# RWKV attention with a mixture of experts: five units' x on ScalarE and GpSimd, and eight half splits of w1 moved later

## The chip, the cores and the metric

The kernel runs on one core of one Trainium2 chip. The metric is the device time of one execution in microseconds (us); the time of a kernel is the median of several runs.

## The reference

First a linear recurrence per head (4 batches, 8 heads, 768 steps, head size 48), then a top-1 mixture of 8 experts on its output (3072 tokens of 384 columns, hidden size 1024):

```
y[t]  = r[t] . (state + (u*k[t]) outer v[t]);   state = w[t]*state + k[t] outer v[t]
x     = y as (tokens, 384)
e     = argmax(x @ w_gate + modality_bias[modality_id]);   g = its softmax value
out   = g * (relu(x @ w1[e]) @ w2[e])
```

## The kernel before

**The recurrence.** The 3072 tokens are 24 units of 128 tokens (6 per batch). `att_iter(i)` (L281) is one turn of a software pipeline over i = -2 to 23, called at L831: it prepares unit i+2 (two scans on VectorE at L289 and L292; two products on GpSimd, K at L240 and G at L300; r copied into PSUM by ScalarE at L234 and multiplied on VectorE at L237), does the scores and the state of unit i+1 (TensorE transposes K at L314, ScalarE copies the result to KT at L316, TensorE forms the scores pS at L338, VectorE masks them into A at L340, TensorE computes G's row sums at L271 into the tile pT, ScalarE rescales the state at L246 and L249), and forms y of unit i in the PSUM tile pY (L365, L377, L380). With i it also turns the finished y of unit i-1 into x (`x_rows`, L403), and transposes x of unit i-2 for the gate's logits (`x_cols`, L427 and ScalarE's copy xT at L428; `logits`, L433).

Each engine runs its own instructions strictly in the order in which the program issues them, so a wait of one holds up everything behind it on that engine. Order is set by hand; there is no planner.

**x_rows** adds two terms: y in PSUM and dV in SBUF (GpSimd's product of L296). It has two forms. By default VectorE adds them in one instruction (L417). With `by_two`, which only iterations 2 and 3 use before the change, ScalarE copies y to SBUF (L414) and GpSimd adds dV in place (L415), since the addition reads SBUF alone.

**The splits.** Each expert matrix is used as a sum of two reduced-precision parts: `wh` is the rounded copy (ScalarE), `wl` the rest (raw minus wh, on GpSimd or VectorE). For the first block of tokens, whose expert e0 is known early, w1 is loaded in 8 pieces (L843) into `raw[0]` and split in 16 halves by `w_split_half(n)` (L225): half n belongs to piece n // 2, and is one ScalarE cast of 128x192 (L228) and one GpSimd subtraction (L229). Before the change two halves are done in each of the iterations 7 to 10 (pieces 0 to 3), four in iteration 22 and the last four after iteration 23.

**The experts.** Tokens are scattered to rows sorted by expert (L632) and worked on in blocks of up to 512 (`seq`, L891; the loop at L892). For a block q and each of the 8 pieces f, `blk_up` (L696) runs nine 512-column matmuls (L702) on piece f of wh[0] and wl[0] into one of two PSUM tiles, pS0 and pS1, in turns (q = 0), then a relu on ScalarE (L711) and the rest on VectorE (L713); the tile is free for piece f+2 when both have read it. `blk_down` (L717) follows. Between the pieces, `w_split` (L220) splits the matrices to come: a cast of two pieces on ScalarE (L222) and a subtraction on VectorE or GpSimd (L223).

**The load of the second block.** `blk_raw(1, 0)` (L863) loads the second block's w1 into `raw[0]` in two halves (pieces 0 to 3, pieces 4 to 7), issued by SyncE. It reads the expert's number and a flag from a table (L643, L644), which VectorE finishes with L572; the loads carry that flag as a condition and move nothing if the expert is that of the block before, but are issued, and are waited for, all the same. Whatever reads a part of `raw[0]` after them in the program waits for the load of that half.

```
        if i == NU - 1:
            for n in done:
                w_split_half(n)
...
    blk_raw(1, 0)
...
        for f in range(FC):
            s = 2 * FC * q + f
            blk_up(q, f)
            if q == 0 and f % 2 == 0:
                w_split(1, f // 2)
            if q != 1 and f % 2 and nxt < HO:
                w_split(0, f // 2)
```

Of the kernel before, what the change touches and what calls it, by code (L numbers as in the profile page):

```python
# [20 lines left out]
NU = B * NCH  # L21
# [37 lines left out]
def kernel(ctx: ExitStack, tc: tile.TileContext, rkw, vt, wf, cst, mid, wg, bias, w1, w2, out):  # L59
# [165 lines left out]
    def w_split_half(n):  # L225
        f, c = n // 2, n % 2 * (DM // 2)
        part = lambda t: t[:, f, c:c + DM // 2]
        nc.scalar.copy(out=part(wh[0]), in_=part(raw[0]))  # L228
        nc.gpsimd.tensor_tensor(out=part(wl[0]), in0=part(raw[0]), in1=part(wh[0]).bitcast(F32), op=ALU.subtract)  # L229
# [46 lines left out]
    hooks = []  # L276
    done = iter(range(2 * FC))

    SPLITS = {**{i: 2 for i in range(7, 11)}, NU - 2: 4}

    def att_iter(i):  # L281
        a, m, z = i + 2, i + 1, i
# [15 lines left out]
        if ok(a):  # L298
            mk_k(a, k)
            nc.gpsimd.tensor_tensor(out=wt(a, "G", [P, 512]), in0=r, in1=k, op=ALU.mult)  # L300
        for _ in range(SPLITS.get(i, 0)):
            w_split_half(next(done))
        if ok(z - 1):
            x_rows(z - 1, i in (2, 3))
        last = first(m + 1)
        if ok(m):
            K, R, v = T["K", m], T["R", m], T["v", m]
# [95 lines left out]
    def x_rows(n, by_two=False):  # L403
        c, j = part(n)
        if j == 0:

            T["xp", c] = (rt if c else xa).tile([P, NJS[c], 400], F32, tag="xp", name=f"xp{c}", bufs=1)
        if n == 0:
            T["R"] = pt("x", "pR")

            nc.tensor.matmul(out=T["R"][:, 511:512], lhsT=wm[:, 0:P], rhs=wm[:, 0:1], start=True, stop=True, skip_group_check=True)
        x, dV = T["xp", c][:, j, 0:DM], T["dV", n].rearrange("p a b -> p (a b)")
        if by_two:
            nc.scalar.copy(out=x, in_=T["py", n][:, 0:DM])  # L414
            nc.gpsimd.tensor_tensor(out=x, in0=x, in1=dV, op=ALU.add)  # L415
        else:
            nc.vector.tensor_tensor(out=x, in0=T["py", n][:, 0:DM], in1=dV, op=ALU.add)  # L417

    def part(n):
        c = n >= CUT[1]  # L420
        return int(c), n - CUT[c]
# [274 lines left out]
    def blk_up(q, f):  # L696
        xh, xo = (t[:, :, 0:width(q)] for t in X["x", q][0:2])
        pp = pt(f"u{q}_{f}", UPB[(q * FC + f) % 3] if isinstance(q, int) and q else f"pS{f % 2}", (P, BT))[:, 0:width(q)]
        n = 0
        for c in range(KC):  # L700
            for wsrc, xsrc in ((wh, xh), (wh, xo), (wl, xh)):
                nc.tensor.matmul(out=pp, lhsT=wsrc[0][:, f, c * P:(c + 1) * P], rhs=xsrc[:, c], start=(n == 0), stop=(n == 3 * KC - 1))  # L702
                n += 1
        w = width(q)
        h2 = bp["h"].tile([P, 2 * BT], F32R, tag="h2", name=f"h{q}_{f}", bufs=FC)
        hh, hl = h2[:, 0:w], h2[:, BT:BT + w]
        cuts = ((0, w, BT),)
        if w % P:
            wf = w - w % P
            cuts = ((wf, w, w), (0, wf, BT))  # L710
        nc.scalar.activation(out=hh, in_=pp, func=AF.Relu)  # L711
        for c0, c1, o in cuts:
            nc.vector.scalar_tensor_tensor(out=h2[:, o:o + c1 - c0], in0=pp[:, c0:c1], scalar=0.0, in1=hh[:, c0:c1].bitcast(F32), op0=ALU.max, op1=ALU.subtract)  # L713
        X["h", q, f] = (hh, hl)
        X["hx", q, f] = h2
# [103 lines left out]
    for i in range(-2, NU):  # L819
        if 2 <= i < 7:  # L820
            hooks.append((setup_a, setup_b, setup_c, setup_d, setup_e)[i - 2])
        if i == CUT[1] + 1:
            ra, tb = route_a(0), table(0)
            hooks.extend([lambda: list(ra), lambda: hook_b(0)])
        if i == CUT[1] + 2:
            route_x(0)
        if i >= NU - 2:
            hooks.append(lambda n=1 + 2 * (i == NU - 1): [next(tb, None) for _ in range(n)])
        if i == NU - 1:
            prep.close()  # L830
        att_iter(i)  # L831
        if i == NU - 1:
            for n in done:
                w_split_half(n)
        if i != -1 and ok(i + 3):
            loadv(max(i + 3, 2))
        if ok(i + 6):
            load(i + 6, ((1024, 1541),))
        if i == 4:
            e0 = nc.sync.value_load(e0i[0:1, 0:1], min_val=0, max_val=E - 1)  # L840
        for n in range(2 * FC):
            if i == (n + 4 if n < FC // 2 else NU - 10 + n if n < FC else NU - 6 + (n - FC) // 2):
                w_raw(e0, n // FC, n % FC, parts=FC)  # L843
        if ok(i + 6):
            load(i + 6, ((0, 1024),))
        if i == -1:
            clear((ersb, 0.0), (onesb, 1.0), (one8, 1.0), (mfx, 0.0), (rbx, 0.0))
        if i == 0:
            clear((zt, 0.0), (zt[:, DM:DM + 1], 1.0), (zt[:, DM + 1:DM + 2].bitcast(I32), PAD_ID), (glo, W_LO), (ghi, -W_HI))
            setup_0()  # L850
        if i == 0:
            early()
        if i == 4:
            r0 = nc.sync.value_load(e0r[0:1, 0:1], min_val=0, max_val=(E - 1) * RS)
        if 8 <= i < 8 + JT:
            rows_apart("xz", nc.sync.dma_start(out=xs[ds(r0 + (i - 8) * P, P), :], in_=zt))

        drain(1)
        if i == NU - 3:
            assert not pend  # L860
            blk_load(0)
# [30 lines left out]
    for n, q in enumerate(seq):  # L892
        nxt, nxt2 = (seq[n + d] if n + d < len(seq) else None for d in (1, 2))
        if q >= HO:
            for k in range(2):
                half_up(q, k)
                if n == NQ and k == 0:
                    blk_out(NQ - 1, (JT - 1,))
            if nxt is not None:
                half_t(nxt)  # L900
            half_down(q)
            if nxt is not None:
                blk_out(q, (0,))
            continue

        load = blk_load if nxt < HO else half_load
        if q > 1:
            load(nxt)
        for f in range(FC):
            s = 2 * FC * q + f  # L910
            blk_up(q, f)
            if s == 2:
                logits(NU - 1)
            if q == 0 and f % 2 == 0:
# [3 lines that stand above are left out]
            if s == 4:  # L918
                list(route_a(1))
            if s == 5:  # L920
                route_x(1)
            if s == 6:
                hook_b(1)
            if q == 1 or s == FC - 1:
                drain(1, lambda h: nc.gpsimd.tensor_copy(out=pj, in_=h), X["h", q, f][0])
            if q == 1 and f > 3:
                if f > 4:
                    nc.gpsimd.tensor_copy(out=pj, in_=X["h", q, f][0][0:1, 0:1].bitcast(F32))
                late.pop(0)()
            if q == 1 and f < 2:  # L930
                blk_raw(nxt, f)
            if q == 1 and f == 5:
                assert not pend
                load(nxt)
            tend(s)
        if n == len(seq) - 2:
            bad, end, endh, rest = (nc.values_load(flg[0:1, i:i + 1], min_val=lo, max_val=hi)
                                    for i, lo, hi in ((0, 0, P), (1, NQ, HO), (2, HO + NH, NTAB), (3, 0, P + 1 + NTAB)))
        if q == 0:
            blk_raw(1, 1)  # L940
        if q >= NA and nxt2 is not None:
            blk_raw(nxt2, 0)
        for f in range(FC):
            s = 2 * FC * q + FC + f
            blk_down(q, f)
            if f == 0:
                (blk_t if nxt < HO else half_t)(nxt)
            if q == 1 and f % 2 == 0:
                w_split(0, f // 2)
            if f % 2:  # L950
                w_split(1, f // 2, eng=nc.vector if q in (0, NQ - 1) else None)
            if q == 2 and f in (3, 5):
                next(tab1)
            if q == 0:
                drain(1, lambda h: nc.gpsimd.memset(h, 0.0), X["h", q, f][0])
                if f == 1:
                    tab1 = table(1)
                if f in (1, 4, 6):
                    next(tab1)
                if f == 1:  # L960
                    pad_rows()
            tend(s)
        if q == 1:
            blk_raw(nxt2, 0)
        if q >= 1 and nxt2 is not None:
            blk_raw(nxt2, 1)
        blk_out(q, range(width(q) // P), late=late if q == 0 else None)
        if q == NQ - 1:
            blk_sum(q)
# [190 lines left out]
```

## Time and profile before

| what | value |
|---|---|
| median of 3 runs | 338.92 us (338.17 to 339.05) |
| the profiled execution: its own time | 338.15 us |
| its span in the trace | 336.40 us |
| TensorE (PE) busy | 323.6 us |
| VectorE (DVE) busy | 215.9 us |
| ScalarE (ACT) busy | 204.3 us |
| GpSimd (POOL) busy | 190.7 us |
| recurrence / experts, by the first matmul of line 702 | 0 to 124.1 us / 124.1 us to the end |

The busy times are averages over two stages with different limits: in the recurrence four engines work side by side, in the experts TensorE has nearly all the work. In the rows below, a line of a timeline gives the start in us, the length of one instruction or of several merged ones (x2 and so on), the engine, the line of the program, the operation, and in brackets how long the engine had been idle and what released it.

### The profile page before, as it was taken

Reading aid. Unit: us, or ns where it says so; the run is one execution under the profiler, and the core shown is the slowest. Engines: PE = TensorE matmul, PEld = TensorE weight load, DVE = VectorE, ACT = ScalarE, POOL = GpSimd, SP = SyncE. Lnnn points to the kernel's source line nnn. Section 1 sums busy time; section 2 is a strip of 40 time slices with the busy share of each in tenths; the row PEclk is TensorE's granted clock in tenths of the full one; section 3 lists DMA queues with packets and bytes.
Section 4 is the critical chain, followed back from the end, with each engine's and each line's share of the span. In section 5 each row is a group of like instructions: output and inputs, shape, how many; then the busy total and the mean of one; then the engine's idle time right before and its main releaser. Section 6 shows DMA issues by size and latency. Waiting matters only on the chain. (4 is left out here: it accounts for less than half of the span.)

```text
span 336.4 us, 10136 instructions
## 1 busy us (share of the span) xinstructions
PE 323.6 (96%) x3943; PEld 293.6 (87%) x3943; DVE 215.9 (64%) x381; ACT 204.3 (61%) x462; POOL 190.7 (57%) x221
## 2 busy tenths in 40 slices
PE   7999999999999999999999999999999999999993
PEld 3788989988899897899889988997899889999993
DVE  6999999999999655795333965933560464054230
ACT  3997799787498845542521867638745855642150
POOL 7989889689999925676461680255024703450041
PEclk9999999999999999999999999999999999999998
DMA  7998898877998432425346037026544773260010
GB/s 252 410 362 247 268 305 261 276 249 224 302 312 247 154 92 96 94 95 214 142 146 184 0 82 250 0 72 169 183 166 164 205 239 96 94 211 5 0 74 31
DMA packets 35586, 58.66 MB, mean 174 GB/s; under 512 B 17297, under 2 KB 22089, under 8 KB 35528
## 3 DMA queue, kind: packets, MB, share of 16 engines
q1 hardware_dynamic: 32424, 48.45, 45.8%
q0 software_dynamic: 3104, 9.47, 7.5%
q8 instruction: 33, 0.54, 0.7%
q14 instruction: 25, 0.20, 0.2%
HBM read 57.86 MB, written 12.67 MB: 210 GB/s over the span
## 5 line engine op out<-in xcount | busy, mean ns | idle before, releaser
L223 POOL TENSOR_TENSOR wl<-raw,wh 128x768 fp32r<-128x768 f32 x20 | 38.9, 1951 | 74.8 <-ACT wh L222 74.7
L222 ACT CAST wh<-raw 128x768 fp32r<-128x768 f32 x48 | 39.3, 832 | 38.9 <-PE pU_d L724 23.0
L713 DVE SCALAR_TENSOR_TENSOR h<-pS_u,h 128x512 fp32r<-128x512 f32 (+2 forms) x39 | 23.1, 608 | 39.3 <-ACT h L711 39.0
L744 POOL DMA_INDIRECT out<-ot,xg x24 | 24.3, 1011 | 30.7 <-ACT ot L753 25.2
L702 PE MATMUL pS_u<-xh,wh 128*128 128x512 f32 (+1 forms) x102 | 39.8, 390 | 0.8 <-DVE h L713 0.8
L223 DVE TENSOR_TENSOR wl<-raw,wh 128x768 fp32r<-128x768 f32 x28 | 31.0, 1113 | 14.6 <-ACT wh L222 14.3
L702 PE MATMUL pS_u<-xo,wh 128*128 128x512 f32 (+1 forms) x102 | 39.2, 384 | 0.0
L702 PE MATMUL pS_u<-xh,wl 128*128 128x512 f32 (+1 forms) x102 | 39.2, 384 | 0.0
L711 ACT ACTIVATE h<-pS_u 128x512 fp32r<-128x512 f32 (+1 forms) x34 | 19.7, 586 | 27.7 <-PE pS_u L702 25.6
L724 PE MATMUL pX_d<-wh,h 128*128 128x384 f32 x96 | 32.3, 337 | 0.0
L724 PE MATMUL pY_d<-wh,h 128*128 128x384 f32 x96 | 32.2, 335 | 0.0
L724 PE MATMUL pK_d<-wh,h 128*128 128x384 f32 x96 | 32.1, 334 | 0.0
L240 POOL TENSOR_TENSOR K<-in,B 128x512 f32<-128x512 f32 x24 | 28.5, 1186 | 6.1 <-PE pK L314 2.3
L632 POOL DMA_INDIRECT xs<-xp,posT x24 | 26.1, 1089 | 9.5 <-issue 7.1
L300 POOL TENSOR_TENSOR G<-in 128x512 f32<-128x512 f32 x24 | 30.6, 1276 | 0.0
L289 DVE TENSOR_TENSOR_SCAN B<-in,pX_d 128x516 f32<-128x516 f32 x24 | 29.3, 1219 | 1.7 <-DMA in<-rkw 1.7
L292 DVE TENSOR_TENSOR_SCAN E<-in,pX_d 128x516 f32<-128x516 f32 x24 | 29.5, 1229 | 0.8
L724 PE MATMUL pU_d<-wh,h 128*128 128x384 f32 x80 | 26.7, 334 | 0.0
L713 DVE SCALAR_TENSOR_TENSOR h<-pT_u,h 128x512 fp32r<-128x512 f32 (+2 forms) x17 | 9.5, 576 | 24.2 <-ACT h L711 24.2
L380 PE MATMUL pY<-v,A 128*64 128x48 f32 x368 | 25.1, 222 | 0.0
L246 ACT ACTIVATE pU_st<-pU_st,B 128x48 f32<-128x48 f32 x80 | 22.0, 275 | 2.8 <-PE pU_st L352 0.4
L380 PEld LDWEIGHTS pY<-v,A 128*64 128x64 f32 x368 | 23.7, 138 | 0.0
(237 smaller groups left out, 861.6 us busy)
## 6 DMA issues: line engine op xcount, KB each, us to landing
raw<-w SPq DMA_DIRECT2D x24, 768.0 KB
in<-rkw SPq DMA_DIRECT2D x23, 512.0 KB
v<-vt SPq DMA_DIRECT2D x24, 288.0 KB
in<-rkw SPq DMA_DIRECT2D x23, 258.5 KB
wg<-wf SPq DMA_DIRECT2D x8, 576.0 KB
xl<-xs SPq DMA_DIRECT2D x20, 192.0 KB
raw<-w SPq DMA_DIRECT2D x16, 192.0 KB
xs<-zt SPq DMA_DIRECT2D x12, 193.0 KB
```

Of the source, the lines that this page charges most:

```text
L222: nc.scalar.copy(out=wh[k][:, sl], in_=raw[k][:, sl])
L223: (eng or (nc.vector, nc.gpsimd)[k]).tensor_tensor(out=wl[k][:, sl], in0=raw[k][:, sl], in1=wh[k][:, sl].bitcast(F32), op=ALU.subtract)
L240: nc.gpsimd.tensor_tensor(out=wt(a, "K", [P, 4, P]), in0=quarters(k), in1=quarters(T["B", a][:, 1:517])[:, :, 1:129], op=ALU.mult)
L289: nc.vector.tensor_tensor_scan(out=Bt[:, 516:0:-1], data0=w[:, 516:0:-1], data1=d1[:, 516:0:-1], initial=0.0, op0=ALU.mult, op1=ALU.max)
L292: nc.vector.tensor_tensor_scan(out=Et, data0=w[:, 0:516], data1=d1[:, 1:2].to_broadcast([P, 516]), initial=1.0, op0=ALU.mult, op1=ALU.max)
L300: nc.gpsimd.tensor_tensor(out=wt(a, "G", [P, 512]), in0=r, in1=k, op=ALU.mult)
L380: nc.tensor.matmul(out=yh[64:P, g, sw, hh], lhsT=A[:, hh, g, 1 + sw], rhs=vs[:, g, hh] if sw else v[:, h * D:(h + 1) * D], start=new and n ...
L632: rows_apart("xs", nc.gpsimd.indirect_dma_start(out=xs[:, :], out_offset=bass.IndirectOffsetOnAxis(ap=posT[:, n:n + 1], axis=0), in_=T["xp ...
L702: nc.tensor.matmul(out=pp, lhsT=wsrc[0][:, f, c * P:(c + 1) * P], rhs=xsrc[:, c], start=(n == 0), stop=(n == 3 * KC - 1))
L713: nc.vector.scalar_tensor_tensor(out=h2[:, o:o + c1 - c0], in0=pp[:, c0:c1], scalar=0.0, in1=hh[:, c0:c1].bitcast(F32), op0=ALU.max, op1=A ...
L724: nc.tensor.matmul(out=X["y", q][j], lhsT=hsrc[:, j * P:(j + 1) * P], rhs=wsrc[1][:, f], start=(f == 0 and n == 0), stop=(last and n == 2))
L744: ins = nc.gpsimd.indirect_dma_start(out=out[:, :], out_offset=bass.IndirectOffsetOnAxis(ap=xg[0:n, j, 1:2].bitcast(I32), axis=0), in_=ot[ ...
```

## The change

Iterations 7 to 11 (which form x of units 6 to 10) use the two-instruction form of `x_rows`. The eight half splits of iterations 7 to 10 go away there. Iteration 22 and the end of the recurrence keep four each, but these are now halves 0 to 7 (pieces 0 to 3); halves 8 to 15 (pieces 4 to 7) are done four behind `blk_up(0, 0)` and four behind `blk_up(0, 1)`. The load of L863 now stands ahead of these eight in the program.

```
-    SPLITS = {**{i: 2 for i in range(7, 11)}, NU - 2: 4}
+    SPLITS = {NU - 2: 4}
+    BY_TWO = (2, 3, 7, 8, 9, 10, 11)
...
         if ok(z - 1):
-            x_rows(z - 1, i in (2, 3))
+            x_rows(z - 1, i in BY_TWO)
...
         if i == NU - 1:
-            for n in done:
-                w_split_half(n)
+            for _ in range(4):
+                w_split_half(next(done))
...
             blk_up(q, f)
+            if s < 2:
+                for _ in range(4):
+                    w_split_half(next(done))
             if s == 2:
                 logits(NU - 1)
```

## Rows read from the trace of the kernel before

**Rows 1.** The page's part 1: busy us (share of the span) xinstructions.

```profile
PE 323.6 (96%) x3943; PEld 293.6 (87%) x3943; DVE 215.9 (64%) x381; ACT 204.3 (61%) x462; POOL 190.7 (57%) x221
```

**Rows 2.** Timeline of VectorE, iterations 7 and 8.

```profile
42.65 1.22 DVE L289 TENSOR_TENSOR_SCAN B<-in,pX_d 128x516 f32<-128x516 f32 x1
...
47.17 1.22 DVE L289 TENSOR_TENSOR_SCAN B<-in,pX_d 128x516 f32<-128x516 f32 x1
...
49.79 0.53 DVE L417 TENSOR_TENSOR xp<-pY,dV 128x384 f32<-128x384 f32 x1
```

**Rows 3.** Timeline of TensorE: iterations 7, 10, 13, 21 and 22.

```profile
43.39 0.66 PE L314 MATMUL pK<-cs,K 128*128 128x128 f32 x4
...
45.35 0.63 PE L271 MATMUL pT<-cs,G 128*64 128x2 f32 x16
...
57.91 0.55 PE L427 MATMUL pT<-cs,xp 128*128 128x128 f32 x3
...
74.93 0.88 PE L365 MATMUL pY<-SPb,R 128*64 128x96 f32 x16 [0.28 <-DVE xp L417]
...
109.75 0.66 PE L314 MATMUL pK<-cs,K 128*128 128x128 f32 x4
...
114.46 0.55 PE L427 MATMUL pT<-cs,xp 128*128 128x128 f32 x3
```

**Rows 4.** Timeline of ScalarE, iterations 7 and 8.

```profile
43.60 0.60 ACT L228 CAST wh<-raw 128x192 fp32r<-128x192 f32 x2
...
44.72 0.48 ACT L428 COPY xT<-pT 128x384 f32<-128x384 f32 x1
...
48.43 0.60 ACT L228 CAST wh<-raw 128x192 fp32r<-128x192 f32 x2
```

**Rows 5.** Timelines of ScalarE and GpSimd, iteration 2, which has the two-instruction form.

```profile
20.42 0.48 ACT L414 COPY xp<-pY 128x384 f32<-128x384 f32 x1
...
23.44 1.01 POOL L415 TENSOR_TENSOR xp<-xp,dV 128x384 f32<-128x384 f32 x1
```

**Rows 6.** Timeline of GpSimd, iteration 7: the two subtractions of its splits.

```profile
46.38 1.15 POOL L229 TENSOR_TENSOR wl<-raw,wh 128x192 fp32r<-128x192 f32 x2
```

**Rows 7.** Timeline of ScalarE: iteration 22, then the first pieces of the experts.

```profile
114.64 1.11 ACT L228 CAST wh<-raw 128x192 fp32r<-128x192 f32 x4
...
126.50 0.60 ACT L711 ACTIVATE h<-pS_u 128x512 fp32r<-128x512 f32 x1 [0.95 <-POOL wl L229]
127.00 0.83 ACT L222 CAST wh<-raw 128x768 fp32r<-128x768 f32 x1
128.49 0.60 ACT L711 ACTIVATE h<-pS_u 128x512 fp32r<-128x512 f32 x1 [0.67 <-PE pS_u L702]
129.52 0.83 ACT L222 CAST wh<-raw 128x768 fp32r<-128x768 f32 x1 [0.43 <-DMA raw<-w]
```

**Rows 8.** Waits of SyncE's queue: us in total, times, longest.

```profile
SPq L643 <- DVE fA L572: 10.6, 1, 10.6
```

**Rows 9.** Timeline of SyncE's queue: the two halves of the load of L863.

```profile
129.43 0.09 SPq L217 DMA_DIRECT2D raw<-w  x1
...
129.96 0.08 SPq L217 DMA_DIRECT2D raw<-w  x1
```

**Rows 10.** Timeline of VectorE, pieces 1 and on of the first block.

```profile
129.12 0.69 DVE L713 SCALAR_TENSOR_TENSOR h<-pS_u,h 128x512 fp32r<-128x512 f32 x1 [0.50 <-ACT h L711]
130.39 0.96 DVE L223 TENSOR_TENSOR wl<-raw,wh 128x768 fp32r<-128x768 f32 x1 [0.58 <-ACT wh L222]
```

**Rows 11.** Timeline of TensorE: the first matmuls of pieces 3 and 4.

```profile
131.39 0.50 PE L702 MATMUL pS_u<-xh,wh 128*128 128x512 f32 x1
...
133.57 0.39 PE L702 MATMUL pS_u<-xh,wh 128*128 128x512 f32 x1
```

**Rows 12.** Timelines of VectorE and GpSimd, splitting at the same time, later in the experts.

```profile
188.55 2.01 DVE L223 TENSOR_TENSOR wl<-raw,wh 128x768 fp32r<-128x768 f32 x1 [0.51 <-ACT wh L222]
...
187.86 1.88 POOL L223 TENSOR_TENSOR wl<-raw,wh 128x768 fp32r<-128x768 f32 x1 [9.63 <-ACT wh L222]
```

## The prediction

> **What bounds the kernel now.** I read the page's busy times first: TensorE is busy for 96% of the span [rows 1]. That alone doesn't say that it is the limit in the recurrence, where matmuls are small and VectorE is full too. So I went to the timelines of the single engines, over the iterations that the change touches, and then over the first microseconds of the experts.
>
> VectorE takes 47.17 - 42.65 = 4.52 us for an iteration, without a gap, and 0.53 us of it is the addition that the change takes away [rows 2]. Read alone, that says that VectorE is the limit and that each iteration of the five would give back 0.53 us. But TensorE is slower still: between 43.39 and 57.91 it does iterations 7, 8 and 9, so 14.52 / 3 = 4.84 us each, where an iteration that nothing disturbs (21) takes 114.46 - 109.75 = 4.71 us [rows 3]. VectorE can be slower or faster than that for an iteration; over a batch it keeps up because TensorE has less to do at a batch's first and last unit.
>
> Why 4.84 and not 4.71 is in ScalarE's timeline: with its two casts of the splits it needs 48.43 - 43.60 = 4.83 us per iteration, back to back [rows 4]. Its copy xT ends at 44.72 + 0.48 = 45.20, and TensorE's next group, L271 into the same PSUM tile, starts at 45.35, right behind it [rows 3, 4]. So in iterations 7 to 9 ScalarE, by way of xT, holds TensorE up by about 0.13 us each. In the experts TensorE is the limit: what holds it up there reaches the end, since it has next to no idle time left there that could take a delay up.
>
> **The change part by part.**
>
> *The x of iterations 7 to 11.* VectorE loses five additions, 5 x 0.53 = 2.65 us [rows 2]. ScalarE loses two casts of 0.60 us together [rows 4] and gains a copy of 0.48 us [rows 5]: 4.83 - 0.60 + 0.48 = 4.71 us, which is just TensorE's own pace. In iteration 11, where there were no casts, the copy is new, but iteration 10 closes a batch, so ScalarE has neither KT nor a state to rescale in it and is ahead. GpSimd gains an addition of 1.01 us [rows 5] and loses two subtractions of 1.15 us [rows 6], so nothing. pY is read earlier than now (the copy stands early in ScalarE's order, VectorE's addition behind both scans), so the write of the next pY waits no longer than before; nothing speaks for a loss here.
>
> What TensorE gets out of it: 14.52 - 3 x 4.71 = 0.39 us from iterations 7 to 9. VectorE, which then runs ahead as far as the scores let it, arrives earlier at iteration 13, where TensorE waited 0.28 us for the addition of L417 [rows 3]; that wait goes too. Sum: **0.7 us gained**. Bounds: 0, if the copy makes ScalarE as late as the casts did; 2.65, if VectorE were the limit after all. I take 0.7, since TensorE's 4.71 us is a measured floor of a full iteration. What is late next is TensorE itself.
>
> *The splits that stay at the end of the recurrence.* Four in iteration 22 and four behind iteration 23, as before, only of other pieces, which were loaded long ago: no change.
>
> *The splits that move behind blk_up(0, 0) and blk_up(0, 1).* Their own work is small: four casts take 1.11 us [rows 7], and TensorE needs some 2 us for a piece. The cost is a wait. In the program the load of the second block's w1 now stands ahead of them, and pieces 4 to 7 are its second half. SyncE reads the table for that load only when VectorE has finished it [rows 8], so the two halves are issued at 129.43 and 129.96 and done at about 130.04 [rows 9]. That even a load that moves nothing is waited for is seen before the change: the cast of pieces 0 and 1 starts at 129.52, right when the first half is done, after a wait of 0.43 us put down to that DMA [rows 7]. Now four casts of pieces 4 and 5 wait for the second half from 127.00 on, and behind them, on the same engine, the relu of piece 1.
>
> Step by step, in the old trace's time (records of ScalarE follow each other some 0.1 us before the end of the one in front: relu 126.50 with 0.60, next 127.00 [rows 7]):
> 1. The four casts start at 130.04 and end at 131.15; the cast for w2 (0.83) ends at 131.98; the relu of piece 1 starts at about 131.9, where it started at 128.49 [rows 7].
> 2. VectorE's part of piece 1 starts 129.12 - 128.49 = 0.63 us behind its relu and takes 0.69 [rows 7, 10]: it ends at 133.22. Only then is pS1 free for piece 3, which TensorE began at 131.39 [rows 11]: **a stall of 1.8 us**.
> 3. Piece 3 takes 133.57 - 131.39 = 2.18 us from such a start [rows 11], until 135.40. Meanwhile ScalarE goes from the relu (next start 132.4) through four casts (133.5) and the cast of pieces 0 and 1 for the next block (134.33). VectorE does the subtraction of that one, 0.96 [rows 10], until 135.3, and then its part of piece 2, 0.69, until 136.0. TensorE's piece 4 needs pS0: it begins at 136.0 and not at 135.40, **0.6 us more**. Against 133.57 that is 2.43 us late, and with a second restart (a first matmul takes 0.50 behind a gap, 0.39 without one [rows 11]) 2.5 us.
> 4. Piece 5 needs the relu of piece 3, which ScalarE can do once TensorE is through with it, at about 135.5: with 0.63 and 0.69 behind it, 136.9, before piece 4 ends at about 138.1. From here on nothing is late. The second four casts, at 132.4, have their load long done, and piece 6 comes two pieces behind piece 4, after 140.
>
> GpSimd has eight subtractions more here, of 1.15 / 2 = 0.58 us each [rows 6], and VectorE's subtraction of step 3 falls among them. Later in the trace, where both engines split at once, VectorE's instruction takes 2.01 us where it takes 0.96 us alone [rows 10, 12]: it ends 0.8 us behind GpSimd's, which began first and ended at 189.74. So step 3 can grow by what is left of one subtraction of GpSimd, 0 to 0.58; I take the middle, **0.3**. The Trainium skill, page "SBUF — State Buffer", section "Who interferes with whom", states it as a rule: a VectorE instruction with two SBUF inputs and a GpSimd instruction that reads SBUF shut each other out, and the one that came second waits for the whole of the first. These rows agree; with it the sum is 2.1, without it 1.8.
>
> **Sum:** 1.8 + 0.6 + 0.1 + 0.3 - 0.7 = **2.1 us slower**. Against the profiled execution's own time that is 338.15 + 2.1 = 340.25. That execution lies 0.77 us under the median of the runs shown, so I put it on the median: 338.92 + 2.1 = **341.0**. A measurement of this kernel can tell about 0.3%, 1.0 us, from no change.
>
> **The rivals.**
>
> *The splits don't wait* (not slower). If the casts of pieces 4 and 5 could go at 127.00, they and the cast for w2 would end at 128.9, the relu of piece 1 would be 0.4 us later than 128.49, VectorE's part would end at 130.2 and piece 3 would begin at 131.39 as now. Then only the gain is left: 338.92 - 0.7 = 338.2, no change. It decides from the point where the load is done before 127.7. For it: the two issues are only 0.08 and 0.09 us long [rows 9]. Against: the wait of 0.43 us [rows 7], and the flag that comes from VectorE's last table instruction. Chance 0.12.
>
> *VectorE is the limit of the recurrence*, and all of 2.65 us comes back, at the same stall of 2.8: 338.92 + 0.15 = 339.1, no change. For it: VectorE has no gap in 4.52 us. Against: 4.71 us of TensorE. If in part, between 339.1 and 341.0. Chance 0.09 for what ends below 1.0 us.
>
> *Both at once*: 338.92 - 2.65 = 336.3, faster. Chance 0.04.
>
> *The copy is no cheaper than the casts*: gain 0 and 2.8 of stall, 341.7; this is still my case, and its upper end with 0.3 more for the shut-out is 342.0.
>
> **How the numbers follow.** My case has 0.75, with a range of its own from the first stall alone less the gain, 338.92 + 1.8 - 0.7 = 340.0, to 342.0. For 8 in 10 the range goes down past the second rival's 339.1 toward the first, and takes 0.4 more above for the spread of the runs shown: 338.6 to 342.4. Slower 0.75, same 0.19 (first rival 0.12, second rival's part 0.07), faster 0.06 (the third, and 0.02 of the others' spread).
>
> **What would show it.** Right: in the changed kernel TensorE's iterations 7 to 9 take 4.71 us; the first cast of L228 in the experts follows the second load's issue, with the DMA as what released it; TensorE has an idle stretch of about 1.8 us ahead of piece 3, put down to VectorE's L713, and another of about 0.6 ahead of piece 4; from piece 5 on its times are the old ones, later by what was lost. Wrong: casts of L228 that start right behind the relu of piece 0, TensorE without idle time ahead of piece 3, or an iteration of the recurrence well under 4.7 us.

## The result, and the profile after

The changed kernel takes 341.5 us (median of 22 runs, 340.0 to 344.17); the kernel before, run beside it, 338.99 us (22 runs). The ratio is 1.0075, with a 95% interval of 1.0057 to 1.0092: 2.5 us slower, 1.9 to 3.1. The forecast was 341.0 us, 2.1 us slower. The profiled execution took 340.0 us, with a span of 338.2 us.

The page of the changed kernel, part 1 and two rows of part 2 (the span in 40 slices of 8.5 us):

```profile
PE 325.2 (96%) x3942; PEld 294.9 (87%) x3943; DVE 214.7 (63%) x376; ACT 205.8 (61%) x467; POOL 196.3 (58%) x226
...
PE   7899999999999997999999999999999999999994
...
PEclk9999999999999998999999999999999999999999
```

The counts are the edit's: five instructions fewer on VectorE, five more on ScalarE and on GpSimd [rows 1]. TensorE is busy for 1.6 us more with the same work, and slice 16 (126.8 to 135.3 us, early in the experts) is the one in which a lower granted clock goes with less busy time.

**The recurrence** became shorter. The timeline of TensorE in the changed kernel, the starts of iterations 7 to 10, the start of iteration 12 and its scores, the matmul of iteration 13 that had waited for VectorE's addition, iteration 14, and the first matmul of pieces 0, 2, 3, 4 and 5 and of the first `blk_down`:

```profile
43.31 0.66 PE L315 MATMUL pK<-cs,K 128*128 128x128 f32 x4
...
48.02 0.66 PE L315 MATMUL pK<-cs,K 128*128 128x128 f32 x4
...
52.66 0.66 PE L315 MATMUL pK<-cs,K 128*128 128x128 f32 x4
...
57.31 0.55 PE L428 MATMUL pT<-cs,xp 128*128 128x128 f32 x3
...
65.81 0.66 PE L315 MATMUL pK<-cs,K 128*128 128x128 f32 x4
...
66.72 1.46 PE L339 MATMUL pS<-R,K 64*64 64x128 f32 x32
...
73.95 0.88 PE L366 MATMUL pY<-SPb,R 128*64 128x96 f32 x16
...
75.68 0.66 PE L315 MATMUL pK<-cs,K 128*128 128x128 f32 x4
...
122.86 0.50 PE L703 MATMUL pS_u<-xh,wh 128*128 128x512 f32 x1
...
127.45 0.50 PE L703 MATMUL pS_u<-xh,wh 128*128 128x512 f32 x1 [0.22 <-DVE h L714]
...
129.72 0.52 PE L434 MATMUL pR_x<-cs,xT 128*64 128x8 f32 x12
132.06 0.70 PE L703 MATMUL pS_u<-xh,wh 128*128 128x512 f32 x1 [1.81 <-DVE h L714]
132.56 0.63 PE L703 MATMUL pS_u<-xo,wh 128*128 128x512 f32 x1
132.99 0.63 PE L703 MATMUL pS_u<-xh,wl 128*128 128x512 f32 x1
...
135.81 0.40 PE L703 MATMUL pS_u<-xh,wh 128*128 128x512 f32 x1
...
137.89 0.39 PE L703 MATMUL pS_u<-xh,wh 128*128 128x512 f32 x1
...
144.74 0.33 PE L725 MATMUL pY_d<-wh,h 128*128 128x384 f32 x1
```

The same marks in the timeline of the kernel before (iterations 12 and 14, piece 0, the first `blk_down`):

```profile
66.59 0.66 PE L314 MATMUL pK<-cs,K 128*128 128x128 f32 x4
...
76.66 0.66 PE L314 MATMUL pK<-cs,K 128*128 128x128 f32 x4
...
124.08 0.50 PE L702 MATMUL pS_u<-xh,wh 128*128 128x512 f32 x1
...
142.46 0.33 PE L724 MATMUL pY_d<-wh,h 128*128 128x384 f32 x1
```

Iterations 7 to 9 take 57.31 - 43.31 = 14.00 us against 14.52 [rows 3]: 4.71, 4.64 and 4.65. The wait of 0.28 at iteration 13 is not in this profile: the row at 73.95 has no bracket. That is not the change's doing, as other profiles show (section on the prediction). From iteration 7 to iteration 14 TensorE needs 75.68 - 43.31 = 32.37 us, against 76.66 - 43.39 = 33.27 before: **0.9 us gained**. The experts begin 1.2 us earlier; I don't count the rest of that, since behind iteration 14, as in iteration 12, TensorE has idle time of a size that differs from one execution to the next and that nothing in the profile explains (last section).

**The experts** lost it, and more. From piece 0 to `blk_down` TensorE needs 144.74 - 122.86 = 21.88 us, against 142.46 - 124.08 = 18.38: **3.5 us lost**. `blk_down` is 2.28 us later than before, and so is every block behind it. The last instruction, GpSimd's output of L745, starts 2.27 us later too, at 334.12 against 331.85. (The spans differ by 1.8 only because what follows that instruction, where no engine works, was 0.5 us longer in the profile of the kernel before.) All of it lies ahead of piece 5: 137.89 - 122.86 = 15.03 us, where it was 11.53 before. The rows show two losses: an idle stretch of 1.81 us ahead of piece 3, and a piece 3 that takes 135.81 - 132.06 = 3.75 us instead of 2.18 [rows 11], its matmuls 0.43 us apart where those of piece 4 are (137.89 - 135.81) / 9 = 0.23 apart.

Why TensorE waited is in the timeline of ScalarE in the changed kernel (the relu of piece 0, the casts of pieces 4 to 7 in two groups of four, the casts for w2, the relus of pieces 1 and 2):

```profile
125.28 0.60 ACT L712 ACTIVATE h<-pS_u 128x512 fp32r<-128x512 f32 x1 [0.96 <-POOL wl L229]
128.94 1.11 ACT L228 CAST wh<-raw 128x192 fp32r<-128x192 f32 x4 [3.06 <-DMA raw<-w]
129.96 0.83 ACT L222 CAST wh<-raw 128x768 fp32r<-128x768 f32 x1
130.70 0.59 ACT L712 ACTIVATE h<-pS_u 128x512 fp32r<-128x512 f32 x1
131.18 1.10 ACT L228 CAST wh<-raw 128x192 fp32r<-128x192 f32 x4
132.18 0.83 ACT L222 CAST wh<-raw 128x768 fp32r<-128x768 f32 x1
132.92 0.59 ACT L712 ACTIVATE h<-pS_u 128x512 fp32r<-128x512 f32 x1
```

The four casts of pieces 4 and 5 wait 3.06 us for the load of L863, whose two halves SyncE issues from 128.27 on and which moves nothing:

```profile
128.27 0.61 SPq L217 DMA_DIRECT2D raw<-w  x2
```

Behind the casts in ScalarE's order stands the relu of piece 1, at 130.70; VectorE's part follows, and piece 3 starts when that ends, at 132.0. The timeline of VectorE, and GpSimd's subtraction that runs beside VectorE's:

```profile
131.31 0.69 DVE L714 SCALAR_TENSOR_TENSOR h<-pS_u,h 128x512 fp32r<-128x512 f32 x1 [3.92 <-ACT h L712]
133.05 1.18 DVE L223 TENSOR_TENSOR wl<-raw,wh 128x768 fp32r<-128x768 f32 x1 [1.04 <-ACT wh L222]
134.15 0.68 DVE L714 SCALAR_TENSOR_TENSOR h<-pS_u,h 128x512 fp32r<-128x512 f32 x1
...
131.58 1.82 POOL L223 TENSOR_TENSOR wl<-raw,wh 128x768 fp32r<-128x768 f32 x1
```

The slow piece 3 is a matter of the clock. Busy time by stretch in the changed kernel (busy us and count of PE, PEld, DVE, ACT and POOL, then the granted clock, the DMA share and GB/s), for the wait and for piece 3:

```profile
129.72:132.06 2.34, 0.53 (x13) 0.43 (x13) 0.69 (x1) 2.34 (x8) 2.34 (x5) 1.00 0.93 331
132.06:135.55 3.49, 3.49 (x9) 2.75 (x10) 1.78 (x2) 2.17 (x4) 3.49 (x4) 0.52 0.46 113
```

0.52 of full speed is nearly the lower of the two levels, 1.2 of 2.4 GHz. In the first stretch TensorE was busy for 0.53 of 2.34 us; then it ran piece 3 at half speed and came back to full speed at about its end. The Trainium skill, page "TensorE: Matmul & The Clock Gate", section "Wait — 56ns, not 53.3ns?", gives a 512-column matmul 426.7 ns from start to start at the lower level and 215.7 at the upper. The rows agree at the lower one (0.43 us) and are somewhat above it at the upper (0.23 us).

### The profile page after: what moved, and what is told of

The parts are those of the page before. It is cut to its first block, busy times and chain, and to the rows that moved or that the text cites. A ratio compares the mean times of both kernels' runs of the same rounds, so it can differ in the third digit from the quotient of the medians.

```text
span 338.2 us, 10127 instructions
## 1 busy us (share of the span) xinstructions
PE 325.2 (96%) x3942; PEld 294.9 (87%) x3943; DVE 214.7 (63%) x376; ACT 205.8 (61%) x467; POOL 196.3 (58%) x226
## 3 DMA queue, kind: packets, MB, share of 16 engines
q1 hardware_dynamic: 32424, 48.45, 45.8%
## 5 line engine op out<-in xcount | busy, mean ns | idle before, releaser
L223 POOL TENSOR_TENSOR wl<-raw,wh 128x768 fp32r<-128x768 f32 x20 | 38.9, 1954 | 69.6 <-ACT wh L222 69.5
L703 PE MATMUL pS_u<-xh,wh 128*128 128x512 f32 (+1 forms) x102 | 40.5, 397 | 2.6 <-DVE h L714 2.6
L745 POOL DMA_INDIRECT out<-ot,xg x24 | 24.3, 1013 | 30.7 <-ACT ot L754 25.2
L223 DVE TENSOR_TENSOR wl<-raw,wh 128x768 fp32r<-128x768 f32 x28 | 32.0, 1148 | 15.1 <-ACT wh L222 14.8
L703 PE MATMUL pS_u<-xo,wh 128*128 128x512 f32 (+1 forms) x102 | 40.0, 392 | 0.0
L703 PEld LDWEIGHTS pS_u<-xh,wh 128*128 128x128 f32 x102 | 19.5, 191 | 6.9 <-DVE h L714 3.5
L341 DVE TENSOR_TENSOR A<-pS,m 128x768 f32<-128x768 f32 x24 | 22.8, 949 | 2.1 <-PE pS L339 1.7
```

The costliest lines, as they stand in the source:

```text
L223: (eng or (nc.vector, nc.gpsimd)[k]).tensor_tensor(out=wl[k][:, sl], in0=raw[k][:, sl], in1=wh[k][:, sl].bitcast(F32), op=ALU.subtract)
L745: ins = nc.gpsimd.indirect_dma_start(out=out[:, :], out_offset=bass.IndirectOffsetOnAxis(ap=xg[0:n, j, 1:2].bitcast(I32), axis=0), in_=ot[ ...
```

## The experiments

Eight kernels. The theory: the second block's load now holds up the splits, these hold up the relu of piece 1, and the idle time that this gives TensorE brings the slow clock; less a gain of 0.7 to 0.9 us in the recurrence. The rivals: the splits' own work costs the time, or the new split of x does. All ratios are to the kernel before (338.71 us median of 25 runs beside the first four, 338.68 of 35 beside the last four), and all changes are made to the changed kernel except in the fourth. Ratios and intervals are those on record; they are not the quotients of the medians, and differ from these by up to 0.5 us.

**No second load.** The two halves of the load of L863 are left out.

```
-        for half in range(2):
+        for half in range(0 if (q, k) == (1, 0) else 2):
```

> The changed kernel without the two w1 loads of the second block (they move nothing here, since that block has the first block's expert). Theory, the moved casts wait for that load: the casts of pieces 4 and 5 follow the relu of piece 0 at once, no idle time of TensorE ahead of piece 3, no stretch at half clock in piece 3, and only the recurrence's gain is left: 1.2 us faster than before (ratio 0.9965), 3.5 us faster than the changed kernel. Rival, the eight casts and subtractions themselves are too much for ScalarE and GpSimd at the start of the experts: the stall ahead of piece 3 stays, about 2 us slower than before.

338.06 us, ratio 0.9994 (0.9976 to 1.0011): 0.2 us faster than before (0.8 faster to 0.4 slower). The wait is gone, and with it the stall and the slow clock. That the load moves nothing shows in the page's part 3: queue q1 has 32424 packets with it and without it. The timeline of ScalarE in this kernel:

```profile
125.83 0.60 ACT L712 ACTIVATE h<-pS_u 128x512 fp32r<-128x512 f32 x1 [0.96 <-POOL wl L229]
126.32 1.10 ACT L228 CAST wh<-raw 128x192 fp32r<-128x192 f32 x4
...
128.06 0.59 ACT L712 ACTIVATE h<-pS_u 128x512 fp32r<-128x512 f32 x1
```

The same eight casts stand in the same place and TensorE needs 18.57 us from piece 0 to `blk_down`, 0.19 more than before. So the work of the splits is nearly free there, and nearly the whole of the 3.5 us hangs on the wait. Most of the 0.19 is lost ahead of piece 6, which waits for VectorE: it starts at 137.04, 0.28 us behind the matmul in front where 0.23 is usual, and with the restart that is 0.16 us. The timelines of VectorE and GpSimd in this kernel:

```profile
134.46 1.92 DVE L223 TENSOR_TENSOR wl<-raw,wh 128x768 fp32r<-128x768 f32 x1
136.31 0.68 DVE L714 SCALAR_TENSOR_TENSOR h<-pS_u,h 128x512 fp32r<-128x512 f32 x1
...
133.72 1.84 POOL L223 TENSOR_TENSOR wl<-raw,wh 128x768 fp32r<-128x768 f32 x1
```

The subtraction takes 1.92 us where it takes 0.96 alone [rows 10], while GpSimd does its own of L229 and L223. The expected 1.2 us was missed: it had counted the experts' earlier start in one profile as gain.

**The load behind the splits.** `blk_raw(1, 0)` and what follows it for block 1 move from ahead of the first block to behind the splits of `blk_up(0, 1)`.

```
-    blk_raw(1, 0)
...
             if s < 2:
                 for _ in range(4):
                     w_split_half(next(done))
+            if s == 1:
+                blk_raw(1, 0)
...
```

> The changed kernel with the second block's w1 load, the write of the padding rows and the load of the second block's rows moved in the program behind the eight moved splits. Theory, the order of load and splits is all: as without the load, 1.2 us faster than before (within 0.3). Rival 1, the work itself: about 2 us slower than before. Rival 2, the load now waits for GpSimd's last subtraction and the second block comes late: the stall moves to the second block's start, 0 to 2 us slower than before.

338.23 us, ratio 0.9989 (0.9963 to 1.0016): 0.4 us faster than before (1.3 faster to 0.5 slower), where 1.2 was expected, for the same reason as without the load. From piece 0 to `blk_down` 18.59 us, no wait of the casts and the clock at its upper level: the order alone repairs it, with all the work left in. The second rival, a late second block, did not come: from `blk_down` to TensorE's next wait, in a later block, are 232.35 - 142.76 = 89.59 us, and before 232.05 - 142.46 = 89.59.

**The splits moved, x as before.**

```
-    BY_TWO = (2, 3, 7, 8, 9, 10, 11)
+    BY_TWO = (2, 3)
```

> The splits moved as in the change, but x of iterations 7 to 11 by VectorE as before. Theory, ScalarE's casts held TensorE up in iterations 7 to 9 and VectorE only at iteration 13: TensorE's iterations 7 to 9 take 4.71 us and not 4.84, the wait at iteration 13 stays, so the experts begin 0.4 us earlier than before and not 1.2, and the loss there is the same 3.5: 3.1 us slower than before. Rival, the gain came from VectorE's lost additions alone: nothing gained, 3.5 us slower than before.

341.61 us, ratio 1.0079 (1.0055 to 1.0104), 2.7 us slower than before (1.9 to 3.5). The experts show the changed kernel's loss again, 21.90 us from piece 0 to `blk_down`, with the same 1.81 us and the same clock. The first matmul of piece 3 in the timeline of TensorE:

```profile
133.21 0.53 PE L703 MATMUL pS_u<-xh,wh 128*128 128x512 f32 x1 [1.81 <-DVE h L714]
```

and piece 3 by stretch:

```profile
133.21:136.95 3.74, 3.74 (x10) 2.92 (x11) 1.78 (x2) 2.17 (x4) 3.74 (x5) 0.54 0.43 105
```

Its iterations 7 to 9 take 14.29 us, between 14.52 and 14.00, and from the start of iteration 7 to that of iteration 12 it needs 66.23 - 43.38 = 22.85 us, against 23.20 before and 22.50 in the changed kernel: losing the casts alone frees ScalarE. The time fits the theory's 3.1, but its interval just reaches the rival's 3.5; it is these starts that speak against the rival. The wait at iteration 13, which was expected to stay, is not in this profile.

**x alone.** The kernel before, with the two-instruction form in iterations 7 to 11 and the splits where they were.

```
-            x_rows(z - 1, i in (2, 3))
+            x_rows(z - 1, i in (2, 3, 7, 8, 9, 10, 11))
```

> Only the x of iterations 7 to 11 by ScalarE and GpSimd, the splits where they were before. Theory, ScalarE sets the pace there: 4.83 + 0.48 less an overlap of 0.1 = 5.2 us in iterations 7 to 9, so 1.1 us lost on TensorE by iteration 10, of which the wait at iteration 13 gives back 0.3 and iterations 10 and 11 perhaps some: 0.3 to 1.0 us slower than before. Rival, VectorE is the limit: 2.2 us faster than before.

340.59 us, ratio 1.0071 (1.0044 to 1.0097), 2.4 us slower than before (1.5 to 3.3), more than expected. The timeline of TensorE, the matmuls L271 of iterations 7 and 8 (9 waits 0.49, 10 waits 0.43):

```profile
47.47 0.63 PE L271 MATMUL pT<-cs,G 128*64 128x2 f32 x16 [0.53 <-ACT xT L428]
...
52.57 0.63 PE L271 MATMUL pT<-cs,G 128*64 128x2 f32 x16 [0.39 <-ACT xT L428]
```

VectorE has 2.65 us less to do, and the recurrence is slower: with copy and casts ScalarE needs 50.54 - 45.34 = 5.20 us an iteration (the casts' starts), and its xT holds TensorE up each time. Iterations 7 to 9 take 15.56 us, 1.04 more than before, which is the size expected of them; 10 and 11 take 0.38 and 0.29 more. That makes 1.7 us; the interval begins just below it, and the two medians differ by 1.9. The 0.3 that the wait at iteration 13 was to give back did not come: TensorE still waits 0.28 us there for VectorE's addition, at 78.18. In its profile the experts take 18.41 us to `blk_down`: they are not touched.

**TensorE kept busy in the wait.** Eight matmuls of 128x512, whose result nothing uses, stand behind the logits ahead of piece 3. They shorten no wait.

```
             if s == 2:
                 logits(NU - 1)
+                fl = pt("fill", "pT")
+                for i in range(8):
+                    nc.tensor.matmul(out=fl, lhsT=wm[:, 0:P], rhs=wm, start=(i == 0), stop=(i == 7))
```

> The changed kernel with eight matmuls of no use (128x512, into a free PSUM tile) on TensorE ahead of piece 3, in the time in which it stood idle for 1.81 us. Theory, the granted clock of 0.52 in piece 3 comes from that idle time: piece 3 runs at full clock in 2.2 us and not 3.75, then piece 4 waits 0.6 us for the relu and the rest of piece 2 (done at 134.83), which the slow clock had hidden: 0.9 us faster than the changed kernel, about 1.4 us slower than before. Rival, the clock falls for another reason (the work of the other engines, the program's code): piece 3 stays at 3.75 us and the time is the changed kernel's, 2.3 us slower than before.

340.46 us, ratio 1.0047 (1.0023 to 1.0071): 1.6 us slower than before and about 1 us faster than the changed kernel, for work added. The intervals of the two overlap, but the profiles agree: from piece 0 to `blk_down` the loss is 2.75 and not 3.50 us. The timeline of TensorE:

```profile
131.27 1.90 PE L920 MATMUL pT_fill<-wm 128*128 128x512 bf16 x8
133.15 0.50 PE L703 MATMUL pS_u<-xh,wh 128*128 128x512 f32 x1
...
135.98 0.50 PE L703 MATMUL pS_u<-xh,wh 128*128 128x512 f32 x1 [0.47 <-DVE h L714]
```

and piece 3 by stretch:

```profile
133.15:135.50 2.35, 2.35 (x10) 1.61 (x9) 1.36 (x2) 2.18 (x4) 2.35 (x2) 1.00 0.20 39
```

So it was the idle time that brought the clock down. With the clock kept up, piece 4 waits for VectorE as the forecast had it. Pieces 0 to 3 take 12.06 us up to piece 4's start, against 133.57 - 124.08 = 9.49 before [rows 11]: 2.57 us, of which 133.15 - 123.92 less 131.39 - 124.08, 1.92, ahead of piece 3.

**Three PSUM tiles for the first block.** `blk_up` takes pS0, pS1 and a third tile in turns in block 0 too, as the later blocks do.

```
-        pp = pt(f"u{q}_{f}", UPB[(q * FC + f) % 3] if isinstance(q, int) and q else f"pS{f % 2}", (P, BT))[:, 0:width(q)]
+        pp = pt(f"u{q}_{f}", UPB[(q * FC + f) % 3] if isinstance(q, int) else f"pS{f % 2}", (P, BT))[:, 0:width(q)]
```

> The changed kernel with three PSUM tiles for the first block's pieces in turns, not two, the load and its wait as they are. Theory, what stopped TensorE is the tile pS1, held by piece 1's late relu: piece 3 takes another tile and starts at once, piece 4 waits some 0.5 us for piece 1's and piece 5 some 0.7 us for piece 2's, short enough that the clock stays: 1 us faster than the changed kernel or more, between 0.3 us faster and 1.0 us slower than before. Rival, ScalarE's lateness costs what it costs wherever it is met: as the changed kernel, 2.3 us slower than before.

338.74 us, ratio 1.0014 (0.9985 to 1.0044): the casts wait their 3.06 us as in the changed kernel, but piece 3 has a tile that is free. The loss from piece 0 to `blk_down` falls from 3.50 to 0.68 us, and the clock stays up. What is left is this stall, ahead of piece 5, and about 0.2 ahead of piece 4:

```profile
135.20 0.50 PE L703 MATMUL pT_u<-xh,wh 128*128 128x512 f32 x1 [0.52 <-DVE h L714]
```

**Both repairs.** The load behind the splits, and three tiles.

> The load behind the splits, as in the second experiment, and three PSUM tiles for the first block. Theory: no wait for the load, and the stall of 0.24 us ahead of piece 2 and that of 0.28 us ahead of piece 6 go too: 0.5 us faster than the second experiment, 0.9 us faster than before (ratio 0.997). Rival, TensorE meets the same waits one piece later: as the second experiment, 0.4 us faster than before.

337.98 us, ratio 0.9975 (0.9952 to 0.9998): 0.9 us faster than before, about what can be told from no change, and faster than the changed kernel. Piece 0 to `blk_down` takes 18.19 us, less than before, because the wait of 0.2 us ahead of piece 2, which the kernel before has too, is gone (0.5 us up to the start of piece 4, of which 0.3 is lost again ahead of piece 7). The 0.28 us ahead of piece 6 in the expectation is the distance of two starts; the stall was 0.05 us and a restart of 0.11. Against the second experiment the size is the theory's, but the intervals overlap. Its profile has an unexplained stall of 1.11 us in the recurrence, with a slow clock behind it (last section).

**The splits one piece later.** The two groups of four stand behind `blk_up(0, 1)` and `blk_up(0, 2)`; the load is where the change has it.

```
-            if s < 2:
+            if s in (1, 2):
```

> The changed kernel with its eight moved splits one piece later, behind pieces 1 and 2, the load where it is. Theory, the cost is the relu of piece 1 queued behind casts that wait for the load: now that relu goes first, the casts wait 1.2 us behind it, the relu of piece 2 is about 0.9 us late, and TensorE idles 0.3 us ahead of piece 4 at most: 0.4 us faster than before (between 0.7 faster and 0.2 slower). Rival, the casts' wait costs its length wherever they stand: 1 us or more slower than before.

338.07 us, ratio 0.9991 (0.9968 to 1.0014), as expected. The timeline of ScalarE:

```profile
127.03 0.60 ACT L712 ACTIVATE h<-pS_u 128x512 fp32r<-128x512 f32 x1 [0.68 <-PE pS_u L703]
128.69 1.11 ACT L228 CAST wh<-raw 128x192 fp32r<-128x192 f32 x4 [1.06 <-DMA raw<-w]
```

The casts still wait for the load, until the same step of SyncE, but the relu of piece 1 stands ahead of them and is on time. The experts lose 0.40 us and not 3.50: a wait of ScalarE costs little by itself here; what was queued behind it did.

**All kernels together.** The time from piece 0 to `blk_down` in each profile against the change of the measured time (ratio less 1, times the median of before). The difference of the two is what the measured time says of everything else, in the main the recurrence.

| kernel | piece 0 to blk_down, us over 18.38 | measured time, us against before | left for the recurrence |
|---|---|---|---|
| the change | +3.50 | +2.5 | -1.0 |
| no second load | +0.19 | -0.2 | -0.4 |
| load behind the splits | +0.21 | -0.4 | -0.6 |
| TensorE kept busy | +2.75 | +1.6 | -1.2 |
| three tiles | +0.68 | +0.5 | -0.2 |
| both repairs | -0.19 | -0.9 | -0.7 |
| one piece later | +0.40 | -0.3 | -0.7 |
| splits moved, x as before | +3.52 | +2.7 | -0.8 |
| x alone | +0.03 | +2.4 | +2.4 |

The seven kernels with the change's recurrence give 0.2 to 1.2 us of gain, 0.7 in the mean; a single row is uncertain by 0.6 to 1.0 us. (By the differences of the medians they give 0.5 to 1.0, 0.8 in the mean.) The eighth row gives as much, 0.8, without the new x: by the measured times, how much of the gain is x's and how much comes from the casts' leaving is not settled. The traces say a little more. From the start of iteration 7 to that of iteration 12 TensorE takes 23.20 us before and 22.85 with the casts gone alone. With the new x as well it takes 22.50 to 22.67 in the five profiles in which no unexplained stall falls into that stretch (22.87 and 23.30 in the two with one, of 0.22 and 0.53). So there the casts' leaving gives about 0.35 us and the new x 0.2 to 0.35 more; for the kernel without the new x that is a single profile.

## Why the prediction was right, and where it was not

**What bounds the recurrence: right for the iterations that the change touches.** TensorE and ScalarE, not VectorE. Two rivals had VectorE as the limit; "x alone" takes 2.65 us from VectorE and is slower. In the changed kernel VectorE waits for TensorE instead; only from iteration 10 on has it next to no gap, and at iteration 13 TensorE waits for it (next paragraph). Its timeline, iteration 8 (iteration 9 waits 0.48):

```profile
49.91 0.96 DVE L341 TENSOR_TENSOR A<-pS,m 128x768 f32<-128x768 f32 x1 [0.54 <-PE pS L339]
```

The waits are about the 0.53 us that it no longer works [rows 2].

**The gain of the recurrence: right in size, not in its parts.** The forecast was 0.39 us from iterations 7 to 9, by a floor of 4.71 us, and 0.28 at iteration 13. The iterations gave 0.52 (0.36 to 0.52 in the six profiles with this recurrence that have no unexplained stall there), since some of them took 4.64 and 4.65: the iteration taken as undisturbed was none.

At iteration 13 VectorE's addition comes earlier, as forecast, but it still decides when TensorE goes on. TensorE's matmul starts 0.06 us behind its end before the change (74.93 behind 74.87) and in the changed kernel (73.95 behind 73.89). The wait is missing there only because TensorE had stopped for some 0.56 us in the scores of iteration 12 (the row at 66.72 takes 1.46 us; without a stop it is 0.90). Without the load there is no such stop, and the wait is back, in the timeline of TensorE:

```profile
74.45 0.88 PE L366 MATMUL pY<-SPb,R 128*64 128x96 f32 x16 [0.28 <-DVE xp L418]
```

It is there with 0.28 us too with the load behind the splits and with TensorE kept busy. So what is gained by iteration 14 hangs on this addition: 0.9 us in the changed kernel, 0.52 without the load, 0.1 to 0.9 in the seven profiles with this recurrence (0.6 in the mean; in two of them, with three tiles and one piece later, TensorE comes 0.2 us behind the addition), and 0.22 with x as before. Here, unlike in iterations 7 to 9, VectorE's lost work counts, and the rival that has VectorE as the limit was right in part. That 0.39 and 0.28 add up to the 0.7 of the measured times is in part luck.

**The load that moves nothing is waited for: right.** This decided the case, and the first rival with it (the splits don't wait, no change). Forecast 3.04 us for the casts (127.00 to 130.04), measured 3.06. The first stall was forecast as 1.8 us and measured 1.81.

**The second stall: right, but another loss took its place.** Forecast were 0.6 us ahead of piece 4, 0.1 for a second restart and 0.3 for VectorE's subtraction beside GpSimd's. In the changed kernel none of them shows, because the step before them failed: "piece 3 takes 2.18 us from such a start". It took 3.75, 1.57 more, at the lower clock. VectorE's part of piece 2 is done at 134.83, before the slow piece 3 ends, so piece 4 has nothing left to wait for. With the clock kept up, the sum comes as forecast: up to the start of piece 5, behind which the forecast had nothing late, 138.19 - 123.92 = 14.27 us in the kernel with the eight matmuls, against 135.61 - 124.08 = 11.53 before (starts of pieces 0 and 5), or 2.74 us where 2.8 was the sum. The clock's own price in the changed kernel is then 3.50 - 2.75 = 0.75 us: 1.57 more for piece 3, less the second stall and its restart that it hides. The prediction had seen an idle stretch of 1.8 us coming and had given it no price beyond its length; its bounds had no term for it.

**The subtraction beside GpSimd's: right in kind, its bound too small.** It took 1.18 us in the changed kernel, hidden under piece 3, and 1.92 without the load, where it held up piece 6. Both times it began beside a subtraction of GpSimd's that had begun first, and ended 0.83 and 0.82 us behind its end (133.40 and 135.56), as in rows 12 (190.56 behind 189.74). The rule cited in the prediction, from the Trainium skill, page "SBUF — State Buffer", section "Who interferes with whom", agrees with these rows. But what stood in front was a subtraction of L223, of 1.8 us, and not one of L229, of 0.58: the bound of 0.58 was too small, and without the load 0.96 us were added.

**The sum.** 2.8 - 0.7 = 2.1 was forecast; 3.5 in the experts, less 0.7 to 1.0, makes 2.5 to 2.8, where 2.5 (1.9 to 3.1) was measured. The range, 338.6 to 342.4, holds it. The term that was too small is the loss in the experts, by the 0.7 us of the clock, which had no term. That the miss stayed so small is in part luck: the slow piece 3 cost 1.57 us and hid 0.82 of what had been forecast.

## What to carry to other kernels

Before a reader is moved down in a program, look which writers it passes, conditional loads that move nothing included: here eight cheap casts cost the experts 3.5 us because a load, ready 3 us later, now stood ahead of them. A wait on an engine that works in order is priced by what stands behind it: one relu behind the casts made nearly the whole loss, and putting it ahead of them, or a third buffer, took nearly all of it away. And an idle stretch of TensorE isn't priced by its length alone: read the granted clock behind it.

## What was not expected of the hardware

**The clock behind a stall.** An idle stretch of 1.81 us, in a stage where TensorE had run at the upper level until then, was followed by 3.5 us at 0.52 of the clock, and at 0.54 in the kernel with the splits alone moved. With eight matmuls in the same stretch the clock stayed at 1.00, and with three tiles, where the longest stall in the first block is 0.52 us, too.

**Stalls that nothing explains.** In all ten profiles TensorE stops in the row sums L271 of iteration 15, put down to "issue", for 0.46 to 1.11 us, in most of them again in iteration 16, and in some once earlier. These are as large as the gain studied here. The longest ones also show that the length of a stall doesn't tell its price. The rows behind three of them, first in the timeline of TensorE with the load behind the splits:

```profile
89.28 0.34 PE L271 MATMUL pT<-cs,G 128*64 128x2 f32 x5 [1.14 <-issue]
```

in that of x alone:

```profile
29.63 0.39 PE L352 MATMUL pU_st<-v,KT 128*48 128x48 f32 x8 [1.34 <-issue]
```

and in that of both repairs:

```profile
83.82 0.57 PE L271 MATMUL pT<-cs,G 128*64 128x2 f32 x13 [1.11 <-issue]
```

Behind the first two the granted clock stays at 1.00. Behind the third, the shortest, it is 1.00 up to 85.20 us and 0.57 from there to 89.20. Why they come, and why only one of the three was followed by the slow clock, was not found.
